# Decayed attention, a top-1 expert layer and a gated layer: three small edits that move work between VectorE, ScalarE and GpSimd

## The chip, the cores and the metric

The kernel runs on one core of a Trainium2 chip. The metric is device time of one execution in microseconds (us), as the median of three runs; lower is better. TensorE is called PE below, VectorE DVE, ScalarE ACT, GpSimd POOL and SyncE SP, as in the rows of the profile. PEld is the load of weights into TensorE, which runs beside its matmuls.

## The reference

Three layers follow one another. Sizes: B=4, H=8, S=576, D=64, so 2304 tokens of 512 numbers; 8 experts of width 1024; a gated layer of width 1536.

```python
def _attn_ref(q, k, v, f):
    scores = np.matmul(q, k.transpose(0, 1, 3, 2)) / np.sqrt(D)
    cum = np.cumsum(np.log(np.clip(f, 0.0001, 1.0)), axis=-1)
    scores = np.where(causal, -1000000000.0, scores + cum[:, :, :, None] - cum[:, :, None, :])
    return softmax(scores) @ v

def _moe_ref(x, modality_id, w_gate, modality_bias, w1, w2):
    logits = x @ w_gate + modality_bias[modality_id]
    e_idx = np.argmax(logits, axis=1)
    gate_w = softmax(logits)[np.arange(N), e_idx]
    for e in range(E):
        mask = e_idx == e
        out[mask] = gate_w[mask, None] * (np.maximum(x[mask] @ w1[e], 0.0) @ w2[e])

def _moe2_ref(x, w_gate, w_val, w_out):
    return (1.0 / (1.0 + np.exp(-(x @ w_gate))) * (x @ w_val)) @ w_out
```

## The kernel before

**Attention.** 32 heads are worked through one after the other, as 16 pairs. A head's step has scores on PE, a sum with the decay and a maximum on DVE (L249), exponentials on ACT (L257), transposes of the probabilities on PE (L268, L271), their high part on ACT (L278) and the low part on DVE (L279), the product with v (L336) and the sum over it that makes the rows of x and the logits (L367, L369, L550 on DVE, L551 on POOL). Matmuls work on a high and a low part of each number, so that each fp32 operand is split: a copy to the high part, then a subtraction for the low part. POOL builds the decay of the next head (`mask`, L183 and L187), and splits q, k and v of later heads (L147 to L167).

**Routing.** When the first half of the tokens has its logits (head 16 on), `early` picks two experts: `choose(0)` and `choose(1)` take the expert with most tokens, count at most 256 of them (`n`), and take them off the counts (`cnt`); `slots`, `ids` and `fetch` place these tokens and gather their rows. `finish` places all the others after the last head, with `place` called for all 18 token tiles (n == NTILE); `place` makes `hot`, a one-hot of the group, and `am`, `hot` times the tile's index and times the row's index, which a matmul with `bm` turns into lists of ids.

**Experts.** A unit is up to 256 tokens of one expert. Its weights come as 8 pieces of 128x1024, piece 2i from w1, piece 2i+1 from w2. `high` (L915 on POOL, L917 on ACT) and `low` (L923 on POOL or DVE) split a piece. Unit 0 uses buffers that attention leaves (`spare`): in rows of the trace eqd, ekd, esc, eph, epl are raw pieces or results of relu, and eq, ekh, ekl, edec are high and low parts. `pair` runs `up(f)` on PE (L989), `relu` (ACT L959 the high part, DVE L960 the low part) and, one step later, `down(f)` (L999). `up(f)` needs piece 2(f//2), `down(f)` piece 2(f//2)+1 and the result of relu f. In unit 0 the code splits pieces 0 to 3 in `begin` and pieces 4 to 7 in `step0`, and `POOL0` lists the pieces that POOL splits. Unit 1 follows with weights `ws`, split on ACT and DVE (wh, wl).

**What sets the order.** All of this up to unit 0 and `finish` is put in order by a scheduler when the program is built, from the order of the code and from its own estimates of when each operand is there; every engine then runs its list in order. From `rest` on the order is that of the code (`manual_schedule`).

Of the kernel before, what the change touches and what calls it, by code (L numbers as in the profile page):

```python
# [14 lines left out]
AF = mybir.ActivationFunctionType  # L15
ALU = mybir.AluOpType
# [4 lines left out]
P = 128  # L21
# [3 lines left out]
NTILE = NT // P  # L25
# [432 lines left out]
class Routing:  # L458
# [147 lines left out]
    def place(self, slot, add, g, ids):  # L606

        nc, V, tmp, n = self.nc, self.nc.vector, self.tmp, slot.shape[1]
        pi = tmp.tile([P, 3, n], I32, tag="pi", name="pi")
        dg = tmp.tile([P, 2, n], F32, tag="dg", name="dg")  # L610
        bm = tmp.tile([P, n, P], BF16, tag="bm" if n == NTILE else "xh0", name="bm")
        hot = tmp.tile([P, n, g], BF16, tag="hot", name="hot")
        am = tmp.tile([P, n, 2, g], BF16, tag="am", name="am")
        V.tensor_scalar(pi[:, 2], slot, add, None, ALU.add)
        V.tensor_scalar(pi[:, 0], pi[:, 2], 7, None, ALU.arith_shift_right)
        V.tensor_scalar(pi[:, 1], pi[:, 2], P - 1, None, ALU.bitwise_and)
        V.tensor_copy(dg, pi[:, 0:2])

        def onehot(o, digit, lanes):
            V.tensor_tensor(  # L620
                o, digit.unsqueeze(2).to_broadcast(o.shape), lanes.unsqueeze(1).to_broadcast(o.shape), ALU.is_equal
            )

        onehot(hot, dg[:, 0], self.grp[:, 0:g])
        nc.gpsimd.tensor_tensor(am[:, :, 0], hot, self.tix[:, 0:n].unsqueeze(2).to_broadcast([P, n, g]), ALU.mult)
        V.tensor_scalar(am[:, :, 1], hot, self.pix, None, ALU.mult)
        for i in range(0, n, 9):
            onehot(bm[:, i:i + 9], dg[:, 1, i:i + 9], self.lane)

        def collect(ps):  # L630
            for i in range(n):
                nc.tensor.matmul(ps, bm[:, i], am[:, i], start=(i == 0), stop=(i == n - 1))
            im = tmp.tile([P, 2, g], F32, tag="im", name="im")
            nc.scalar.activation(im, ps, AF.Copy)
            V.scalar_tensor_tensor(ids, im[:, 0], float(P), im[:, 1], ALU.mult, ALU.add)

        return collect

    def early(self):

        nc, V, wp = self.nc, self.nc.vector, self.wp
        t = lambda name, shape: wp.tile(shape, F32, tag=name, name=name)
        flat = lambda z: z.rearrange("p e o -> p (e o)")
        n0e, st = flat(self.n0e), {}

        def count():
            ps = self.ps_t.tile([P, 2, E, HT], F32, tag="t", name="t")
            st["rk"], st["cnt"] = self.ranks(ps, HT)

        def choose(i):  # L650

            cnt, mx, em, ne = flat(st["cnt"]), t("mx0", [P, 1]), t("em0", [P, 1]), t("ne0", [P, E])
            es, n = flat(self.es[i]), self.n0[:, i:i + 1]
            V.tensor_reduce(mx, cnt, AX.X, ALU.max)
            V.tensor_scalar(n, mx, 2.0 * P, None, ALU.min)
            V.tensor_scalar(es, cnt, n, None, ALU.is_ge)
            V.tensor_tensor(es, es, self.desc, ALU.mult)
            V.tensor_reduce(em, es, AX.X, ALU.max)
            V.tensor_scalar(es, self.desc, em, None, ALU.is_equal)
            V.tensor_scalar(self.te0[:, i:i + 1], em[0:1], -1.0, float(E), ALU.mult, ALU.add)  # L660
            ne = ne if i else n0e
            V.tensor_scalar(ne, es, n, None, ALU.mult)
            V.tensor_tensor(cnt, cnt, ne, ALU.subtract)
            if i:
                V.tensor_tensor(n0e, n0e, ne, ALU.add)

        def slots():

            rk, sel, off = st["rk"], t("sel", [P, E, HT]), t("off0", [P, E, 1])
            V.tensor_tensor(sel, rk, self.n0e.to_broadcast([P, E, HT]), ALU.is_lt)  # L670
            V.tensor_tensor(sel, sel, self.oh[:, :, 0:HT], ALU.mult)
            V.tensor_tensor(off, self.es[1], self.es[0], ALU.is_gt)
            V.tensor_scalar(off, off, 2.0 * P, -2.0 * P * NE, ALU.mult, ALU.add)
            V.tensor_tensor(rk, rk, off.to_broadcast([P, E, HT]), ALU.add)
            V.tensor_tensor(rk, rk, sel, ALU.mult)
            rr = t("rr", [P, HT])
            V.tensor_reduce(rr, rk.rearrange("p e t -> p t e"), AX.X, ALU.add)
            st["collect"] = self.place(rr, 2.0 * P * NE, 2 * NE, self.ids0)

        def ids():  # L680
            st["collect"](self.ps_t.tile([P, 2, 2 * NE], F32, tag="t", name="t"))
            pad, row = t("pad0", [P, 2]), t("row0", [P, 2])
            first, n = self.slot[:, 0:2], self.nt
            V.memset(n, 0.0)
            for i in range(NE):
                V.tensor_scalar(pad, first, self.n0[:, i:i + 1], None, ALU.is_ge)
                V.tensor_scalar(row, first, n, None, ALU.add)
                V.scalar_tensor_tensor(self.dst0[:, 2 * i:2 * i + 2], pad, float(2 * NT), row, ALU.mult, ALU.add)
                V.tensor_tensor(n, n, self.n0[:, i:i + 1], ALU.add)

        def fetch():
            for i, x in enumerate(self.xg):
                nc.gpsimd.indirect_dma_start(
                    out=x[:, :], out_offset=None, in_=self.xd[0:NT // 2],
                    in_offset=bass.IndirectOffsetOnAxis(ap=self.ids0[:, i:i + 1], axis=0),
                )

        return [count] + [lambda i=i: choose(i) for i in range(NE)] + [slots, lambda: None, ids, fetch] + self.then

    def finish(self, tmp, ps):  # L700
# [99 lines left out]
        V.tensor_tensor(row, self.slot, flat(of[:, 0]), ALU.add)  # L800
        V.scalar_tensor_tensor(self.dst, pad, float(2 * NT), row, ALU.mult, ALU.add)
        return lambda: place(ps.tile([P, 2, G], F32, tag="m", name="t", bufs=1))


class Experts:
# [2 lines left out]
    ORDER = [(0, 0), (1, 0), (0, 1), (1, 1), (0, 2), (1, 2), (0, 3), (1, 3)]  # L808


    POOL0 = 0, 1, 2, 4, 6
    SPARE = {"w": "kqkqcspr", "h": "2ldh2ldh", "l": "hd2lhd2l", "a": "kqkqkqkq"}

    def __init__(self, tc, ro, ps, xd, yd, w1, w2):
# [96 lines left out]
    def high(self, u, p):  # L911
        k = self.piece(u, p)
        hi = self.w[u, k] = self.part(u, p, "h")
        if u == 0 and p in self.POOL0:
            self.nc.gpsimd.tensor_scalar(hi, self.wraw(u, k), 1.0, 1.0, ALU.mult, ALU.mult)  # L915
# [3 lines left out]
    def low(self, u, p):  # L919
        k = self.piece(u, p)  # L920
        hi, lo = self.w[u, k], self.part(u, p, "l")
        eng = self.nc.gpsimd if u == 0 and p in self.POOL0 else self.nc.vector
        ins = eng.tensor_tensor(lo, self.wraw(u, k), hi.bitcast(F32), ALU.subtract)  # L923
# [471 lines left out]
```

## Time and profile before

| what | us |
|---|---|
| median of three runs | 998.96 (997.98 to 999.78) |
| the profiled execution | 1000.64 |
| its span, first to last instruction | 998.9 |
| PE busy in the span | 947.6 |
| DVE, ACT, POOL busy in the span | 576.1, 481.0, 298.3 |

The profiled execution is one run of the kernel, 1.74 us longer than its span and 1.68 us above the median. Times in rows count from the start of the span. Attention runs to about 267 us, unit 0 from there to 296, the other units to about 520, the gated layer to the end. PE has the most work; where it stops, the rows give in brackets how long it was idle and what ended that.

### The profile page before, as it was taken

What the parts mean: (1) busy time and instruction counts of PE and PEld (TensorE: products, weight loads), DVE (VectorE), ACT (ScalarE), POOL (GpSimd) and SP (SyncE); (2) the same over time, 40 slices, a digit from 0 to 9 for tenths busy, and PEclk for the clock granted to TensorE, in tenths of its full rate; (3) what the DMA queues carried; (4) which work ended last, traced back from release to release, by engine and by line L of the source; (5) the groups of instructions that cost most, each with busy time, mean ns of one, the idle gap of its engine ahead of it and who ended that gap; (6) DMA issues with size and microseconds to landing.
All of it is one profiled execution on the core that took longest, in us unless ns stands there. A gap on an engine that the chain in (4) does not pass through costs nothing. (4 is left out here: it accounts for less than half of the span.)

```text
span 998.9 us, 16941 instructions
## 1 busy us (share of the span) xinstructions
PE 947.6 (95%) x5871; PEld 878.9 (88%) x5871; DVE 576.1 (58%) x1494; ACT 481.0 (48%) x1058; POOL 298.3 (30%) x563
## 2 busy tenths in 40 slices
PE   4999999889979999999989998999999999999996
PEld 4899998789868999999879887999999999999995
DVE  7988889888796889898766682122122122122111
ACT  5889888678436666666664442122122122112111
POOL 6999998879422222211000001001001001001001
PEclk8999999999999999999999998999999999999998
DMA  6545547344354394345732220001001001000000
GB/s 141 136 124 132 130 111 135 87 104 157 103 178 128 108 304 137 112 134 176 243 132 75 84 95 32 1 1 64 1 1 64 1 1 64 1 1 32 1 1 32
DMA packets 95486, 88.98 MB, mean 89 GB/s; under 512 B 47456, under 2 KB 78688, under 8 KB 95392
## 3 DMA queue, kind: packets, MB, share of 16 engines
q1 hardware_dynamic: 90752, 73.12, 26.2%
q0 software_dynamic: 4640, 14.70, 4.2%
q8 instruction: 48, 0.79, 0.3%
q14 instruction: 46, 0.38, 0.1%
HBM read 98.72 MB, written 14.77 MB: 114 GB/s over the span
## 5 line engine op out<-in xcount | busy, mean ns | idle before, releaser
L1226 PE MATMUL g<-xh,gh 128*128 128x384 f32 x576 | 195.5, 339 | 3.3 <-PEq L1354 3.1
L1226 PE MATMUL g<-xl,gh 128*128 128x384 f32 x576 | 193.8, 336 | 0.0
L1233 DVE TENSOR_TENSOR s<-s,g 128x384 f32<-128x384 f32 x72 | 39.8, 553 | 257.5 <-PE g L1226 257.5
L1226 PE MATMUL g<-xh,bits 128*128 128x384 f32 x528 | 177.6, 336 | 1.7 <-DVE bits L1175 1.6
L1259 POOL DMA_INDIRECT out_dram<-os,tok x18 | 17.5, 973 | 458.1 <-ACT os L1258 456.3
L1226 PEld LDWEIGHTS g<-xh,gh 128*128 128x128 f32 x576 | 108.6, 189 | 5.9 <-ACTq L1354 3.5
L1234 ACT ACTIVATE ah<-s 128x384 fp32r<-128x384 f32 x72 | 37.8, 525 | 157.5 <-DVE s L1233 157.5
L1226 PEld LDWEIGHTS g<-xl,gh 128*128 128x128 f32 x576 | 108.7, 189 | 1.8
L1232 ACT ACTIVATE s<-g 128x384 f32<-128x384 f32 x72 | 35.3, 490 | 140.2 <-PE g L1226 137.2
L1226 PEld LDWEIGHTS g<-xh,bits 128*128 128x128 f32 x528 | 99.1, 188 | 2.9 <-DVE bits L1175 2.9
L923 DVE TENSOR_TENSOR wl<-ws,wh 128x1024 fp32r<-128x1024 f32 x80 | 97.2, 1216 | 3.3 <-ACT hr L1032 2.3
L257 ACT ACTIVATE sc<-sc,mn 128x576 f32<-128x576 f32 (+4 forms) x160 | 89.3, 562 | 14.0 <-DVE mn L249 13.2
L917 ACT ACTIVATE wh<-ws 128x1024 fp32r<-128x1024 f32 x80 | 84.4, 1056 | 18.7 <-PE y L999 17.2
L1244 PE MATMUL o<-gh,ah 128*128 128x512 f32 x216 | 85.9, 398 | 3.6 <-ACT gh L1174 3.6
L183 POOL TENSOR_SCALAR dec<-cum 128x576 f32<-128x576 f32 (+4 forms) x160 | 84.5, 540 | 4.2 <-DMA cum<-drow 4.0
L1244 PE MATMUL o<-gh,al 128*128 128x512 f32 x216 | 84.7, 392 | 0.0
L969 POOL DMA_INDIRECT rows_by_expert<-ys,dst x20 | 23.8, 1188 | 180.3 <-ACT ys L968 94.4
L989 PE MATMUL h<-xh,wh 128*128 128x256 f32 x256 | 73.9, 289 | 0.0
L1244 PE MATMUL o<-gl,ah 128*128 128x512 f32 x180 | 71.3, 396 | 2.0 <-DVE gl L1175 2.0
L989 PE MATMUL h<-xl,wh 128*128 128x256 f32 x256 | 72.5, 283 | 0.4 <-DVE xl L944 0.4
L989 PE MATMUL h<-xh,wl 128*128 128x256 f32 x256 | 72.6, 284 | 0.0
L279 DVE TENSOR_TENSOR pl<-t,ph 128x512 fp32r<-128x512 f32 x96 | 65.0, 679 | 11.5 <-ACT ph L278 10.7
(301 smaller groups left out, 2364.7 us busy)
## 6 DMA issues: line engine op xcount, KB each, us to landing
ws<-in_moe_w_dram SPq DMA_DIRECT2D x80, 512.0 KB
cum<-drow SPq DMA_DIRECT2D x32, 288.0 KB
raw<-in_moe_w_gate_dram SPq DMA_DIRECT2D x12, 512.0 KB
raw<-in_moe_w_val_dram SPq DMA_DIRECT2D x12, 512.0 KB
raw<-in_moe_w_out_dram SPq DMA_DIRECT2D x12, 512.0 KB
y<-rows_by_expert SPq DMA_DIRECT2D x18, 256.5 KB
qr<-in_q_dram SPq DMA_DIRECT2D x32, 128.0 KB
kd<-in_k_dram SPq DMA_DIRECT2D x32, 128.0 KB
```

The lines of the kernel that those rows point to most:

```text
L183: nc.gpsimd.tensor_scalar(t[0:m, DO[b]:DO[b] + W[b]], c[0:m, 0:W[b]], -1.0, c[0:m, R0[b]:R0[b] + 1], ALU.mult, ALU.add)
L257: nc.scalar.activation(so, so, AF.Exp, bias=mn[0:m, b:b + 1], scale=-1.0, accum_out=sm[0:m, c:c + 1])
L279: nc.vector.tensor_tensor(pl[0:m, o:o + w], t, ph[0:m, o:o + w].bitcast(F32), ALU.subtract)
L917: self.nc.scalar.activation(hi, self.wraw(u, k), AF.Copy)
L923: ins = eng.tensor_tensor(lo, self.wraw(u, k), hi.bitcast(F32), ALU.subtract)
L969: nc.gpsimd.indirect_dma_start(out=self.put[g], out_offset=bass.IndirectOffsetOnAxis(ap=dst[:, j:j + 1], axis=0), in_=ys[:, :], in_offset= ...
L989: nc.tensor.matmul(t, a[:, c, cs], b[:, c, :], start=(n == 0), stop=(n == 3 * KD - 1))
L1226: nc.tensor.matmul(t, p[:, c, :], q[:, c, :], start=(n == 0), stop=(n == 3 * KD - 1))
L1232: nc.scalar.activation(s, ps[0], AF.Sigmoid)
L1233: nc.vector.tensor_tensor(s, s, ps[1], ALU.mult)
L1234: nc.scalar.activation(hi, s, AF.Copy)
L1244: nc.tensor.matmul(o[j], p[:, cs], q, start=(f == 0 and n == 0), stop=(f == self.NF - 1 and n == 2))
```

## The change

Three edits. In `choose`, the row `ne = es * n` (one number per expert, 128x8) is made by ACT in place of DVE, in both calls. In `place`, the product that makes the first half of `am` is made by DVE in place of POOL when it is called for all 18 tiles; the early call with 9 tiles stays on POOL. And POOL splits pieces 0, 1, 2, 3 of unit 0 where it split 0, 1, 2, 4, 6: piece 3 goes from ACT and DVE to POOL, pieces 4 and 6 from POOL to ACT and DVE.

```diff
         onehot(hot, dg[:, 0], self.grp[:, 0:g])
-        nc.gpsimd.tensor_tensor(am[:, :, 0], hot, self.tix[:, 0:n].unsqueeze(2).to_broadcast([P, n, g]), ALU.mult)
+        (V if n == NTILE else nc.gpsimd).tensor_tensor(am[:, :, 0], hot, self.tix[:, 0:n].unsqueeze(2).to_broadcast([P, n, g]), ALU.mult)
...
             ne = ne if i else n0e
-            V.tensor_scalar(ne, es, n, None, ALU.mult)
+            nc.scalar.activation(ne, es, AF.Copy, scale=n)
             V.tensor_tensor(cnt, cnt, ne, ALU.subtract)
...
-    POOL0 = 0, 1, 2, 4, 6
+    POOL0 = 0, 1, 2, 3
```

The scheduler then orders the lists anew. On DVE in `choose(1)` (rk_3211 is `cnt`; L249 is attention's sum and maximum, L279 the low part of probabilities):

```order
 L660 TENSOR_SCALAR te_77<-em_3499 1x1
 L279 TENSOR_TENSOR pl_142<-t,ph_141 128x512
-L662 TENSOR_SCALAR ne_3500<-es_89,n_90 128x8
-L249 ISA sc_137,mn<-s,dec 64x64
-L249 ISA mn 64x1
 L663 TENSOR_TENSOR rk_3211<-rk_3211,ne_3500 128x8
 L665 TENSOR_TENSOR n0e<-n0e,ne_3500 128x8
+L249 ISA sc_137,mn<-s,dec 64x64
+L249 ISA mn 64x1
 L279 TENSOR_TENSOR pl_142<-t,ph_141 128x512
 L249 ISA sc_137,mn<-s,dec 128x448
```

L662 is gone from the list, and the two subtractions that need its result stand ahead of attention's L249, not behind it.

On POOL at the end of attention (eqd, ekd here are raw pieces 1 and 3, 0 and 2; esc is piece 4, eph piece 6):

```order
 L923 TENSOR_TENSOR edec<-eqd,ekl 128x1024
 L551 TENSOR_TENSOR lg<-lt,lg 128x24
+L915 TENSOR_SCALAR ekh<-eqd 128x1024
+L923 TENSOR_TENSOR ekl<-eqd,ekh 128x1024
 L915 TENSOR_SCALAR edec<-ekd 128x1024
 L923 TENSOR_TENSOR eq_4734<-ekd,edec 128x1024
 L551 TENSOR_TENSOR lg<-lt,lg 128x24 x6
-L915 TENSOR_SCALAR eq_4780<-esc_4703 128x1024
-L923 TENSOR_TENSOR ekh_4782<-esc_4703,eq_4780 128x1024
-L915 TENSOR_SCALAR edec<-eph_4705 128x1024
-L923 TENSOR_TENSOR eq_4834<-eph_4705,edec 128x1024
-L625 TENSOR_TENSOR am<-hot,tix 128x18x27
```

Piece 3 is split between pieces 1 and 2, and after the last L551 POOL has no compute left in unit 0.

On DVE in the middle of unit 0, around relu of f=3 (L960), before:

```order
L766 SCALAR_TENSOR_TENSOR pl_4990<-gs,n0e 128x8
L742 TENSOR_REDUCE tef<-past 1x27
L768 SCALAR_TENSOR_TENSOR pl_4992<-c,gs 128x8
L772 TENSOR_TENSOR rk_4942<-rk_4942,pl_4990 128x144
L746 COPY own<-tef 1x7
L747 COPY own<-tef 1x9
L769 TENSOR_TENSOR pl_4992<-pl_4992,gs 128x8
L923 TENSOR_TENSOR edec<-esc_4704,ekl 128x1024
L960 SCALAR_TENSOR_TENSOR eqd<-h,eqd 128x256
```

and there in the changed kernel:

```order
L766 SCALAR_TENSOR_TENSOR pl_4990<-gs,n0e 128x8
L742 TENSOR_REDUCE tef<-past 1x27
L923 TENSOR_TENSOR edec<-esc_4704,ekl 128x1024
L960 SCALAR_TENSOR_TENSOR eqd<-h,eqd 128x256
L923 TENSOR_TENSOR eq_4834<-eph_4705,edec 128x1024
L746 COPY own<-tef 1x7
L747 COPY own<-tef 1x9
```

The low part of relu f=3 stands five rows of `finish` earlier, and the low part of piece 6 follows it. In the same way relu f=7 now stands ahead of the last rows of `finish` (L793 to L801, the list `dst`), where it stood behind them.

## Rows read from the trace of the kernel before

**Rows 1.** The page's first line, the span.
```profile
span 998.9 us, 16941 instructions
```

**Rows 2.** PE timeline: start us, us, instruction, [idle before <-releaser].
```profile
195.14 1.56 PE L367 MATMUL t<-iw,ot 128*128 128x72 f32 x6 [2.90 <-DVE pl L279]
...
258.84 0.67 PE L367 MATMUL t<-iw,ot 128*128 128x72 f32 x4 [1.51 <-DVE ot L354]
...
281.94 0.73 PE L999 MATMUL y<-ekh,eqd 128*128 128x512 f32 x2 [2.81 <-DVE eqd L960]
...
289.73 0.73 PE L999 MATMUL y<-ekl,eqd 128*128 128x512 f32 x2 [1.90 <-DVE eqd L960]
...
298.64 0.38 PE L989 MATMUL h<-xl,wh 128*128 128x256 f32 x1 [0.41 <-DVE xl L944]
```

**Rows 3.** Stretches: us, busy by engine (count), PEclk granted, DMA share, GB/s.
```profile
192.24:195.14 2.90, 0.01 (x1) 0.00 (x0) 2.90 (x7) 1.45 (x5) 2.14 (x5) 1.00 0.50 129
195.14:202.08 6.94, 6.94 (x34) 6.72 (x34) 4.11 (x23) 3.14 (x9) 4.33 (x12) 0.51 0.21 50
260.05:263.31 3.26, 3.26 (x15) 3.07 (x15) 1.64 (x7) 1.09 (x3) 0.23 (x1) 0.50 0.66 220
290.78:294.18 3.40, 3.40 (x16) 3.22 (x14) 2.65 (x9) 0.60 (x2) 0.00 (x0) 0.51 0.56 199
```

**Rows 4.** A stretch later on, columns as in Rows 3 (PE, PEld, DVE, ACT, POOL).
```profile
320.00:340.00 20.00, 20.00 (x131) 18.11 (x130) 16.08 (x28) 13.28 (x21) 5.39 (x4) 1.00 0.33 106
```

**Rows 5.** DVE timeline around choose(1) and the routing rows after it.
```profile
190.53 3.01 DVE L662 TENSOR_SCALAR ne<-es,n 128x8 f32<-128x8 f32 x1
...
201.37 0.21 DVE L320 RECIPROCAL r<-r 128x9 f32<-128x9 f32 x1 [2.81 <-ACT r L319]
...
217.72 0.89 DVE L686 TENSOR_SCALAR pad<-slot,n 128x2 f32<-128x2 f32 x1
```

**Rows 6.** POOL timeline over the time of L662, and its wait after 200.
```profile
190.69 0.72 POOL L187 TENSOR_SCALAR_AFFINE_SELECT dec<-dec 128x128 f32<-128x128 f32 x3
191.39 0.86 POOL L167 TENSOR_TENSOR vv<-vr,vv 128x320 fp32r<-128x320 f32 x1
...
193.05 0.45 POOL L166 TENSOR_SCALAR vv<-vr 128x320 fp32r<-128x320 f32 x1
...
204.53 0.49 POOL L166 TENSOR_SCALAR vv<-vr 128x320 fp32r<-128x320 f32 x1 [3.94 <-PE m L336]
```

**Rows 7.** ACT timeline: a small row, and the high part of piece 3.
```profile
201.14 0.20 ACT L319 ACTIVATE r<-sm 128x9 f32<-128x9 f32 x1
...
251.60 1.06 ACT L917 ACTIVATE ekh<-eqd 128x1024 fp32r<-128x1024 f32 x1
```

**Rows 8.** DVE timeline: the low part of piece 3, then unit 0.
```profile
255.12 3.40 DVE L923 TENSOR_TENSOR ekl<-eqd,ekh 128x1024 fp32r<-128x1024 f32 x1
...
271.26 2.50 DVE L716 TENSOR_TENSOR cmp<-rk,thr 128x144 f32<-128x144 f32 x1
...
274.69 0.28 DVE L770 TENSOR_TENSOR half<-rk,pl 128x144 f32<-128x144 f32 x1
...
277.11 2.29 DVE L766 SCALAR_TENSOR_TENSOR pl<-gs,n0e 128x8 f32<-128x8 f32 x1
...
280.35 1.21 DVE L923 TENSOR_TENSOR edec<-esc,ekl 128x1024 fp32r<-128x1024 f32 x1
...
285.47 0.66 DVE L620 TENSOR_TENSOR hot<-dg,grp 128x486 bf16<-128x486 f32 x1
...
287.32 2.02 DVE L923 TENSOR_TENSOR ekl<-epl,ekh 128x1024 fp32r<-128x1024 f32 x1
```

**Rows 9.** POOL timeline: the low part of piece 6.
```profile
276.75 2.62 POOL L923 TENSOR_TENSOR eq<-eph,edec 128x1024 fp32r<-128x1024 f32 x1
```

**Rows 10.** Unit 0 from relu f=0 to f=7, columns as in Rows 3.
```profile
268.88:294.42 25.54, 20.83 (x122) 17.94 (x121) 24.49 (x72) 5.54 (x11) 9.19 (x5) 0.93 0.50 140
```

**Rows 11.** The rows for dst, columns as in Rows 3.
```profile
291.46:293.40 1.94, 1.94 (x11) 1.94 (x11) 1.79 (x7) 0.00 (x0) 0.00 (x0) 0.50 0.56 195
```

## The prediction

> **What bounds the kernel now.** I began with the stretches. From 320 us on PE is busy for 20.00 of 20 us at full granted clock [rows 4], and its later waits are between engines that follow PE, so whatever is won before 300 us should reach the end as it is. The loss that this change can touch lies ahead of that, in three places, each found by PE's own idle rows and then by the engine that they name.
>
> Place A, `choose(1)`. PE waits 2.90 us for a low part L279 on DVE [rows 2], and DVE is then in L662, 3.01 us for eight numbers per partition [rows 5]. POOL runs one instruction after the other through that time, from L187 at 190.69 to L166, which ends at 193.50 [rows 6], and L662 ends at 193.54. So DVE stood behind POOL's whole train. After it PE's granted clock is 0.51, near its lower level of 1.2 GHz, for 6.94 us [rows 3]; work at half pace loses half of that, 3.4 us. Place A costs 2.9 + 3.4 = 6.3 us.
>
> Place B, the end of attention. PE waits 1.51 us for L354 on DVE [rows 2], which stands behind the low part of piece 3: 3.40 us [rows 8], where the same operation and shape takes 1.21 at 280.35 [rows 8]. Then 3.26 us at granted clock 0.50 [rows 3] lose 1.6. Place B costs 3.1.
>
> Place C, unit 0. PE waits 2.81 and 1.90 us for low parts L960 on DVE [rows 2], and 3.40 us at 0.51 [rows 3] lose 1.7: together 6.4. DVE is the bound here: from relu f=0 to relu f=7 it is busy for 24.49 of 25.54 us [rows 10]. Part of this is again POOL: L716 takes 2.50 where L770, of the same 144 columns and also with two inputs in SBUF, takes 0.28; L766 takes 2.29 for 8 columns [rows 8] and ends at 279.40, as POOL's low part of piece 6 ends at 279.37 [rows 9]; the low part of piece 7 takes 2.02 against 1.21 [rows 8].
>
> **The change part by part.** *ne on ACT.* It removes L662 from DVE. On ACT it is one small row; the nearest, 128x9, takes 0.20 [rows 7], and ACT has no work while DVE stands. L663 now waits for it, and behind L663 in DVE's list are L665 and attention's L249. Both subtractions read two SBUF inputs, so they can stand behind POOL too. At best each waits for nothing, at worst for the 3 us that L662 waited. I take one POOL row each, by the longest of the train, 0.86 [rows 6], less what is idle between: about 1 us for both, so that PE's wait shrinks from 2.9 to under 1. What follows limits the gain. DVE was idle for 2.81 us at 201 [rows 5] because PE was slow, and POOL for 3.94 us up to 204.53 [rows 6], so the small routing rows of `slots` ran free of it. If all moves up, those rows meet a busy POOL, as L686 does, with 0.89 us for two columns [rows 5]. Bounds for A: nothing (the wait passes to L663) and 6.3. I take 2.6, which is 6.3 less about 1 for the subtractions and less some four such meetings of 0.7 us.
>
> The Trainium skill, page "SBUF — State Buffer", section "Who interferes with whom", says that VectorE contends with GpSimd for one pair of ports when it runs in a 2-port mode or reads two SBUF inputs, and that whoever starts first keeps it for its whole instruction. The lengthened rows of place C agree with that; L662 does not, since it stood behind five and more GpSimd instructions and not one. By the page a wait is worth at most one GpSimd row, so A would come to some 0.8 us and the sum below to 7.8; by the row it is 3.01 us.
>
> *Piece 3 to POOL.* DVE loses 3.40 us and ACT 1.06 [rows 7, 8], at a place where both stand before PE's last head. POOL gets the two instructions ahead of piece 2, a copy and a subtraction, the longer no more than the 2.62 of piece 6 [rows 9]. Pieces 2 and 3 are first read in up(2) and down(2), behind up(0), up(1) and down(0), and these hide it; without that cover up(2) would wait for up to twice 2.62. The bounds for B are nothing (the last head's chain of exponentials, copies and products is as long as the wait that goes) and 3.1 plus the 1 us by which ACT is earlier. I take 3.0.
>
> *Pieces 4 and 6 to ACT and DVE, am to DVE.* ACT gets 2 x 1.06 us, and it is busy for 5.54 of 25.54 there [rows 10]: no cost, unless its waits for a buffer hold the relu behind them. DVE gets 2 x 1.21 for the low parts, and am, for which `hot` with the same 486 elements and two inputs is the nearest row, 0.66 [rows 8]: 3.1 us. POOL has then no compute left, so L716 loses 2.2, L766 at least 2.0 (to L770's 0.28) and the low part of piece 7 0.8: 5.0 us off. By the new order the rows for dst, 1.8 us [rows 11], move behind relu f=7. DVE thus needs 24.5 - 5.0 + 3.1 - 1.8 = 20.8 us where it took 25.5, and relu f=7 comes 4.7 us earlier, with PE's stops, now within that, gone or short. PE alone could win 6.4. But the 1.8 us come back ahead of unit 1's weight splits and of the low part of x that PE awaited at 298.64 [rows 2]: by that 4.7 - 1.8 = 2.9 is left, and by PE's stops alone 6.4 - 1.8 = 4.6. I take 4.0, nearer to the second, since PE's stops end with a stretch at half clock that goes with them. Below both lies nothing, if DVE's rows do not shrink. The weights `ws` of unit 1 are loaded once piece 5 is split and once down(5) is done; both come earlier by the order shown, so SP's queue is no new wait.
>
> **Sum.** 2.6 + 3.0 + 4.0 = 9.6 us. Against the profiled execution's own 1000.64 us (span 998.9 [rows 1] and 1.74 around it) that is 991.0; the profile lies 1.68 above the median of 998.96, and against the median it is 989.4. I say **989.5**.
>
> **The rivals.** *The wait is only handed on.* L663 or a routing row behind it runs into POOL's train as L662 did, and A brings nothing. For it speaks that POOL is busy in the same way around it [rows 6]; against it, that nothing else in the shown rows waits for more than one or two instructions of POOL. The Trainium skill's page, named above, speaks against it as well, with one instruction as the longest wait. The time would be 998.96 - 7.0 = 992.0. Chance 0.17.
>
> *Unit 0 is bound by DVE's own list.* Its rows shrink less, or the rows for dst and two weight splits ahead of unit 1 make PE wait as long as before, with a new stretch at half clock. Then C brings nothing or 1, and A and B stay: 998.96 - 5.6 = 993.4, or up to 992.4. For it speaks that DVE keeps 20.8 us of work there; against it the 5.0 us measured behind POOL. Chance 0.12.
>
> *Little moves.* A and C bring nothing and the last head's chain takes B: 998 to 1000. It needs all three, chance 0.06.
>
> *New trains (slower).* The routing rows after `choose(1)`, which ran while POOL was idle for 3.94 us [rows 6], now stand in a full POOL stream. Each that meets a train as long as L662's costs PE 2.9 us idle and 3.4 at half clock, 6.3. One such meeting is A's gain undone; two cost 12.6 against at most 6.3 + 3.0 + 4.0 = 13.3, no change; from three on, 18.9, the kernel is slower by 5.6: 1004.6. Only one row of the trace is that long at such a place, L662, and L686 with 0.89 is the usual kind. Chance 0.04.
>
> **How the numbers follow.** The forecast has what is left, 0.61, and its own range is 985 to 991.5. The predicted time is its likeliest value. A measurement of this kernel tells about 0.2%, 2 us. Faster by more than that hold the forecast, the first rival and the second: 0.90; same is "little moves": 0.06; slower 0.04. The range reaches down to all that the three places cost, 6.3 + 3.1 + 6.4 = 15.8, with the 1 us more in B and less the 1.8 us that come back, 15.0, so 984.0, and up to the second rival with part of its C lost again, 996; beyond lie the last two rivals, with 0.10, and some 0.08 below or between.
>
> **What the changed profile would show.** For A: L662 on ACT at about 0.2 us, L663 and L665 under 1 us each on DVE, and no idle row of PE over 1 us near 192, nor a stretch at 0.5 behind it. For B: no L923 on DVE before unit 0, L354 behind L279 at once, and PE at full clock up to unit 0. For C: L716 and L766 at 0.3 us or less, low parts of pieces 4 to 7 at 1.21 each on DVE, PE without idle rows over 0.5 us between up(0) and down(7), then a wait of 2 to 3 us for unit 1's xl. That xl matmul, at 298.64 before, should stand at about 289. The prediction is wrong if L716 or L766 are as long with POOL idle, if L663 takes L662's 3 us, or if relu's low parts still hold PE.

## The result, and the profile after

The changed kernel takes **989.18 us** (median of four, 987.4 to 990.08) against 999.37 for the kernel before beside it; ratio 0.9896 (0.9869 to 0.9923). The forecast was 989.5. Run again beside other kernels it took 989.87 of 999.01, ratio 0.9909 (0.9882 to 0.9936). The profiled execution took 987.4 us:

```profile
span 985.7 us, 16946 instructions
```

That is 13.2 us under the span of [rows 1], more than the medians' 10.2: one execution of each kernel is compared here, and both kernels spread by several us. PE's timeline of the changed kernel, which answers to [rows 2]:

```profile
183.75 0.33 PE L271 MATMUL t<-swp,sc 128*128 128x128 f32 x1 [1.37 <-DVE pl L279]
193.73 0.33 PE L271 MATMUL t<-swp,sc 128*128 128x128 f32 x1 [0.94 <-DVE pl L279]
...
201.57 0.28 PE L198 MATMUL t<-idr,qd 128*128 128x128 f32 x1 [0.47 <-DVE kl L204]
206.44 0.89 PE L367 MATMUL t<-iw,ot 128*128 128x72 f32 x6 [0.49 <-DVE kl L204]
...
285.88 0.39 PE L989 MATMUL h<-xl,wh 128*128 128x256 f32 x1 [2.37 <-DVE xl L944]
```

Places B and C are clean: no row of PE waits between 221 and 283 us, where it waited for 1.51, 2.81 and 1.90 us, and the matmul for xl stands at 285.88, where it stood at 298.64. The 2.37 us in front of it are the wait forecast there. Unit 0 on DVE, as in [rows 8]:

```profile
263.19 0.30 DVE L716 TENSOR_TENSOR cmp<-rk,thr 128x144 f32<-128x144 f32 x1
...
267.52 0.14 DVE L766 SCALAR_TENSOR_TENSOR pl<-gs,n0e 128x8 f32<-128x8 f32 x1
...
273.37 1.20 DVE L923 TENSOR_TENSOR ekl<-epl,ekh 128x1024 fp32r<-128x1024 f32 x1
...
278.47 0.66 DVE L625 TENSOR_TENSOR am<-hot,tix 128x486 bf16<-128x486 bf16 x1
```

L716 fell from 2.50 to 0.30, L766 from 2.29 to 0.14, piece 7 from 2.02 to 1.20, and `am` takes the 0.66 that `hot` took. One row more got shorter, L737, which I had not counted; before, on DVE's timeline,

```profile
275.94 1.19 DVE L737 TENSOR_TENSOR past<-grp,gs 128x432 f32<-128x432 f32 x1
```

and in the changed kernel:

```profile
266.94 0.59 DVE L737 TENSOR_TENSOR past<-grp,gs 128x432 f32<-128x432 f32 x1
```

Place A is another matter. `choose(1)` on DVE and POOL of the changed kernel:

```profile
190.24 2.79 DVE L659 TENSOR_SCALAR es<-desc,em 128x8 f32<-128x8 f32 x1
...
193.60 0.14 DVE L663 TENSOR_TENSOR rk<-rk,ne 128x8 f32<-128x8 f32 x1
193.68 0.15 DVE L665 TENSOR_TENSOR n0e<-n0e,ne 128x8 f32<-128x8 f32 x1
```

```profile
190.62 0.72 POOL L187 TENSOR_SCALAR_AFFINE_SELECT dec<-dec 128x128 f32<-128x128 f32 x3
191.31 0.85 POOL L167 TENSOR_TENSOR vv<-vr,vv 128x320 fp32r<-128x320 f32 x1
192.13 0.23 POOL L551 TENSOR_TENSOR lg<-lt,lg 128x24 f32<-128x24 f32 x1
192.34 0.67 POOL L152 TENSOR_SCALAR kd<-kd 128x576 f32<-128x576 f32 x1
```

L663 and L665 (both called subtractions above; L665 is an addition) are free, but L659, three rows ahead of L663, now stands behind the same train of POOL, its rows one right after the other, for 2.79 us. PE's wait is 0.94 us all the same, and no half clock follows it. A stretch at half clock came earlier instead, behind the 1.37 us at 183.75 (stretches, columns as in Rows 3):

```profile
184.00:190.00 6.00, 6.00 (x40) 5.74 (x39) 5.08 (x21) 4.06 (x14) 4.88 (x9) 0.72 0.33 75
193.00:203.00 10.00, 8.78 (x67) 7.92 (x68) 9.40 (x43) 8.02 (x25) 6.18 (x17) 1.00 0.21 56
```

So the total fits and two of its three terms stand; whether the third does, one profile can't say.

### The profile page after: what moved, and what is told of

Same layout as the page of the kernel before. It is cut to its first block, busy times and chain, and to the rows that moved or that the text cites. A ratio compares the mean times of both kernels' runs of the same rounds, so it can differ in the third digit from the quotient of the medians.

```text
span 985.7 us, 16946 instructions
## 1 busy us (share of the span) xinstructions
PE 940.9 (95%) x5871; PEld 872.7 (89%) x5871; DVE 567.4 (58%) x1494; ACT 482.1 (49%) x1061; POOL 291.4 (30%) x560
## 5 line engine op out<-in xcount | busy, mean ns | idle before, releaser
L989 PE MATMUL h<-xl,wh 128*128 128x256 f32 x256 | 72.4, 283 | 2.4 <-DVE xl L944 2.4
L989 PE MATMUL h<-xh,wh 128*128 128x256 f32 x256 | 73.7, 288 | 0.0
L989 PE MATMUL h<-xh,wl 128*128 128x256 f32 x256 | 72.6, 284 | 0.0
L279 DVE TENSOR_TENSOR pl<-t,ph 128x512 fp32r<-128x512 f32 x96 | 65.0, 679 | 11.6 <-ACT ph L278 10.7
```

The costliest lines, as they stand in the source:

```text
L279: nc.vector.tensor_tensor(pl[0:m, o:o + w], t, ph[0:m, o:o + w].bitcast(F32), ALU.subtract)
L989: nc.tensor.matmul(t, a[:, c, cs], b[:, c, :], start=(n == 0), stop=(n == 3 * KD - 1))
```

## Experiments

The theory to be tested was that of the prediction, with A in doubt: three places add up, A by `ne`, B by piece 3, C by pieces 4 and 6. The rival was its first rival, that A's wait is only handed on. All times below are medians beside the kernel before on the same chip; 0.001 of the ratio is 1 us. The ratio, with its 95% interval, is not the quotient of the two medians and can differ from it by up to 1.7 us (piece 6 on POOL). Every edit lets the scheduler order the lists anew, so each run shows its edit together with the new order. For each profile I also took three lengths from the timelines. **S0** runs from ACT's copy of a finished head (L349, at 183.77 in the kernel before) to that at 231.20, five heads on, around `choose(1)`. **S1** runs on from there to the first matmul of unit 0 (L989), and **S2** from that to the first xl of unit 1 on DVE (L944). In the kernel before:

```profile
231.20 0.60 ACT L349 ACTIVATE ot<-o 128x512 f32<-128x512 f32 x1 [0.30 <-PE o L336]
...
266.67 0.36 PE L989 MATMUL h<-xh,eq 128*128 128x256 f32 x1
...
297.89 0.69 DVE L944 TENSOR_TENSOR xl<-x,xh 128x512 fp32r<-128x512 f32 x1 [0.27 <-ACT im L634]
```

and in the changed kernel:

```profile
227.33 0.60 ACT L349 ACTIVATE ot<-o 128x512 f32<-128x512 f32 x1 [0.29 <-PE o L336]
...
258.89 0.37 PE L989 MATMUL h<-xh,eq 128*128 128x256 f32 x1
...
285.14 0.68 DVE L944 TENSOR_TENSOR xl<-x,xh 128x512 fp32r<-128x512 f32 x1
```

| kernel | S0 | S1 | S2 | ratio to before |
|---|---|---|---|---|
| before | 47.43 | 35.47 | 31.22 | 1 |
| `ne` alone | 42.90 | 37.03 | 29.66 | 0.9997 (0.9978 to 1.0015) |
| `am` alone | 45.07 | 37.05 | 28.85 | 0.9973 (0.9951 to 0.9994) |
| piece 3 to POOL alone | 45.13 | 31.54 | 31.25 | 0.9951 (0.9935 to 0.9967) |
| piece 4 off POOL alone | 47.74 | 33.89 | 27.64 | 0.9962 (0.9945 to 0.9980) |
| new list alone | 47.31 | 31.57 | 26.24 | 0.9891 (0.9861 to 0.9921) |
| the same again | 45.13 | 31.56 | 26.24 | 0.9903 (0.9884 to 0.9923) |
| list and `am` | 45.15 | 31.55 | 26.40 | 0.9896 (0.9866 to 0.9927) |
| list and `ne` | 44.29 | 31.54 | 26.09 | 0.9882 (0.9854 to 0.9910) |
| the same again | 45.50 | 31.57 | 26.06 | 0.9892 (0.9873 to 0.9911) |
| changed kernel | 43.54 | 31.56 | 26.25 | 0.9896 (0.9869 to 0.9923) |
| the same again | 44.27 | 31.56 | 26.24 | 0.9909 (0.9882 to 0.9936) |
| changed, piece 6 on POOL | 43.34 | 31.54 | 27.68 | 0.9914 (0.9890 to 0.9939) |
| changed, rows for dst later | 46.66 | 31.53 | 24.14 | 0.9941 (0.9921 to 0.9960) |

A length is read from one execution. S0 of the kernel before and of the changed kernel, columns as in Rows 3 (PE's idle time is the length less PE's busy time):

```profile
183.77:231.20 47.43, 41.88 (x302) 39.34 (x303) 41.88 (x151) 33.17 (x95) 37.52 (x78) 0.89 0.47 111
```

```profile
183.79:227.33 43.54, 39.80 (x302) 36.47 (x303) 40.53 (x150) 32.91 (x96) 36.63 (x75) 0.96 0.50 114
```

 What is left of the span behind S2 is 698.8 to 704.0 us in all rows but the last, with or without the gains ahead of it: so these reach the end, but within a spread of 5 us.

**`ne` alone.**

```diff
-            V.tensor_scalar(ne, es, n, None, ALU.mult)
+            nc.scalar.activation(ne, es, AF.Copy, scale=n)
```

> The kernel before with one edit of the change alone: the chosen row's `ne` on ScalarE. Nothing is left out. My theory: in the kernel before, choose(1) holds up the heads behind it through its DVE row L662 (3.01 us) and the half clock that follows PE's 2.90 us wait; with `ne` on ACT the row takes 0.3 us and PE's wait near 193 falls under 1.5 us without a half clock behind it, so 2.6 to 4 us are gained: about 996 us, ratio 0.996 to 0.998. The rival (the wait is only handed on to the next row that DVE writes while POOL's train runs, and PE waits as long as before): L659 or L663 near 190 to 194 takes the 3 us instead, PE's row at 195 stays at 2.5 us or more, and the ratio is within 0.002 of 1.

It took 999.96 us against 999.85: nothing, as the rival says, though the interval leaves room for 2.2 us. The DVE timeline shows the wait handed on, to L663 here, and PE's timeline what it costs:

```profile
191.94 2.56 DVE L663 TENSOR_TENSOR rk<-rk,ne 128x8 f32<-128x8 f32 x1
```

```profile
195.37 0.89 PE L367 MATMUL t<-iw,ot 128*128 128x72 f32 x6 [1.97 <-DVE pl L279]
202.29 0.28 PE L198 MATMUL t<-idr,qd 128*128 128x128 f32 x1 [0.47 <-DVE kl L204]
207.18 0.89 PE L367 MATMUL t<-iw,ot 128*128 128x72 f32 x6 [0.51 <-DVE kl L204]
```

The wait fell from 2.90 to 1.97, and two new ones of 0.47 and 0.51, behind L204 on DVE, take the place of smaller ones: those of PE's idle times that the view shows, from here to the head at 228, add up to 4.85 us, and from the same place in the kernel before to 5.55. So the idle time won is 0.7 us. In this execution no half clock followed, and S0 is 4.53 us shorter; but the stretch from 250 to 260 was granted 0.80, S1 is 1.56 longer, and the time is no better.

**The new list alone, and the change without `ne`.**

```diff
-    POOL0 = 0, 1, 2, 4, 6
+    POOL0 = 0, 1, 2, 3
```

> The kernel before with the list of p pieces for POOL set to 0, 1, 2, 3 alone; `ne` and `am` stay where they were. Nothing is left out. My theory: this is where most of the gain comes from, the end of attention and unit 0: 6.5 to 8 us, about 992 us, ratio 0.992 to 0.9935, with L716 and L766 in unit 0 at 0.1 to 0.3 us instead of 2.3 to 2.5, the row for L662 at 3 us and PE's half clock behind 195 us as before. The rival (unit 0 is bound by DVE's own list, which p6's and p7's splits make longer): only the attention part is gained, 3 to 4 us, ratio 0.996, and DVE's last split ends as late after f0 as in the kernel before.

> The changed kernel without one edit: `ne` stays on DVE. Nothing is left out. My theory: choose(1) costs what it did before (L662 3 us, PE's wait near 195 us at 2.5 us or more and a half clock behind it), and the rest of the gain stays: 6 to 8 us, about 992.5 us, ratio 0.992 to 0.994. The rival (the wait near choose(1) is handed on anyway): no difference from the changed kernel, ratio 0.9895.

The list alone took 989.91 us and with `am` 989.09: the whole gain, by the ratios 10.9 and 10.4 us and so more than the theories' 6 to 8 (the intervals reach down to 7.9 and 7.3). That leaves no room for the rival of the first, and is what the rival of the second says. In both, L662 stood for 3 us and PE for 2.90 us in `choose(1)` as before.

**`am` alone.**

```diff
-        nc.gpsimd.tensor_tensor(am[:, :, 0], hot, self.tix[:, 0:n].unsqueeze(2).to_broadcast([P, n, g]), ALU.mult)
+        (V if n == NTILE else nc.gpsimd).tensor_tensor(am[:, :, 0], hot, self.tix[:, 0:n].unsqueeze(2).to_broadcast([P, n, g]), ALU.mult)
```

> The kernel before with `am` (the routing product of the last units) on DVE alone. Nothing is left out. My theory: this row, 0.6 to 0.9 us on either engine, decides nothing by itself: ratio within 0.001 of 1. The rival: POOL's `am` is one of the rows behind which DVE's rows of unit 0 wait, and without it up to 1 us is gained, ratio 0.999.

997.23 us, 2.7 less by the ratio (0.6 to 4.9): more than the theory allows, though the interval reaches down to it, and the rival has the mechanism; its 1 us lies in the interval. In the kernel before, POOL's `am` took 2.06 us from 286.21, not the 0.6 to 0.9 that I had put, and DVE's low part of piece 7 beside it 2.02 [rows 8]. Without it, on DVE's timeline:

```profile
289.00 1.22 DVE L923 TENSOR_TENSOR ekl<-epl,ekh 128x1024 fp32r<-128x1024 f32 x1
```

PE's wait of 1.90 us behind it is gone and S2 is 2.37 shorter. But not all of that is the work of `am`. In `ne` alone, where unit 0 has the same list for POOL and the same rows as in the kernel before, S2 is 1.56 shorter too, and that wait is 0.61 on PE's timeline:

```profile
288.24 0.73 PE L999 MATMUL y<-ekl,eqd 128*128 128x512 f32 x2 [0.61 <-DVE eqd L960]
```

There the half clock follows the first of unit 0's two waits (granted 0.60 from 280.47 to 284.00), in the kernel before the second. In `am` alone it follows the first as well (0.59 from 283.64 to 287.20), so the S2 to compare with is that of `ne` alone, and it is 0.81 shorter.

**Pieces 3 and 4, one at a time.**

```diff
-    POOL0 = 0, 1, 2, 4, 6
+    POOL0 = 0, 1, 2, 3, 4, 6
```

> The kernel before with p3 alone moved to POOL: POOL splits p0, p1, p2, p3, p4, p6. Nothing is left out. It is to measure the end of attention by itself. Theory: DVE's 3.40 us for p3's low at 255.12 goes, PE's wait of 1.51 us at 258.84 and the half clock behind it go with it, and unit 0 starts 3 to 4 us earlier; unit 0 itself keeps its waits (L716, L766, PE's 2.81 us): 995.5 to 997 us, ratio 0.996 to 0.997. Rival (the two parts are one wait: unit 0 starts earlier, but its end hangs on DVE and POOL as before, so that PE only waits longer for eqd): under 1 us, ratio 0.999 or more.

```diff
-    POOL0 = 0, 1, 2, 4, 6
+    POOL0 = 0, 1, 2, 6
```

> The kernel before with p4 alone moved to DVE: POOL splits p0, p1, p2, p6. Nothing is left out. It is to measure unit 0 by itself. Theory: L716 comes down from 2.5 to 0.3 us, since POOL's split of p4 no longer runs beside it, DVE's 1.2 us for p4 are less than that, and PE's two waits in unit 0 shrink from 4.7 us to under 2.5 us; the end of attention stays as it was: 994.5 to 996.5 us, ratio 0.995 to 0.997. Rival (only p6's place counts, or DVE's list is the bound): ratio 0.999 or more.

Piece 3 alone took 993.95 us: 4.9 off by the ratio (3.3 to 6.5), more than expected. S1 fell by 3.93 and S2 stayed to 0.03, so B is a place of its own; the waits of unit 0 are all there in PE's timeline:

```profile
275.26 0.73 PE L999 MATMUL y<-ekh,eqd 128*128 128x512 f32 x2 [2.82 <-DVE eqd L960]
```

Piece 4 alone took 996.02 us, 3.8 off (2.0 to 5.5), as expected, and S2 fell by 3.58 (2.02 against `ne` alone). Piece 6, still on POOL, now holds a third row, L748, as the POOL and the DVE timeline show:

```profile
277.09 2.55 POOL L923 TENSOR_TENSOR eq<-eph,edec 128x1024 fp32r<-128x1024 f32 x1
```

```profile
277.31 2.36 DVE L748 TENSOR_SCALAR rev<-own 1x18 f32<-1x18 f32 x1
```

The two together are 8.7 us by the ratios, the list 9.7 to 10.9.

**Piece 6 back on POOL.**

```diff
-    POOL0 = 0, 1, 2, 3
+    POOL0 = 0, 1, 2, 3, 6
```

> The changed kernel with one more piece for POOL: p6 back on it, so that DVE splits p4, p5, p7 and POOL p0, p1, p2, p3, p6. Nothing is left out. Theory: what the new list gives in unit 0 comes from DVE's rows no longer standing behind POOL's split of p6: L766 is 2.2 to 2.4 us long again beside that split, but DVE has 1.2 us less of its own, so the first row of unit 1 for PE comes 0 to 2 us later: 989 to 991 us. Rival (unit 0 is bound by the sum of DVE's rows, and the row that waits costs nothing): it is faster than the changed kernel by 1.2 us, 988 us.

988.75 us, no difference from the changed kernel's 989.87 that could be told, so neither side is decided by the time. S2 is 1.43 longer, by the same 2.4 us in L748 less the 1.2 us that DVE no longer has; L766 was free, against what I expected. The wait fell to the row that DVE came to when POOL's long row had begun: L766 in the kernel before, L748 in these two.

**`ne` within the new list.**

```diff
-        (V if n == NTILE else nc.gpsimd).tensor_tensor(am[:, :, 0], hot, self.tix[:, 0:n].unsqueeze(2).to_broadcast([P, n, g]), ALU.mult)
+        nc.gpsimd.tensor_tensor(am[:, :, 0], hot, self.tix[:, 0:n].unsqueeze(2).to_broadcast([P, n, g]), ALU.mult)
```

This is the changed kernel with `am` back on POOL; the list alone differs from it in `ne` only.

> The changed kernel itself, once more, beside the runs that follow. Nothing is left out. The four runs so far put `ne` alone at no difference and the new list for POOL alone at 0.989, about the whole gain. Theory now: `ne` brings forward the heads behind choose(1) by 3 us or more, but the new list alone has most of the gain, so the changed kernel comes within 1.5 us of the kernel without `ne`: 988 to 990.5 us, ratio 0.989 to 0.991. Rival (the three edits add up, and 3.9 us of choose(1) show in the time): 985 to 986.5 us, ratio 0.986.

> The changed kernel with `am` back on POOL. Nothing is left out. Theory: 0.7 us of POOL's time at 278 us in front of DVE's last rows of unit 0, which PE's wait for unit 1 hangs on; 0 to 1 us over the changed kernel, about 989.8 us. Rival (what `am` alone gave on the kernel before, 2.6 us, is its own worth in either kernel): 991.5 us or more.

> The changed kernel with `am` back on POOL once more, beside the same kernel without `ne` on ACT (the next run): the pair differs in `ne` alone. Nothing is left out. Theory: `ne` is worth about 1 us here, less than the 2 us by which profiles with it come through choose(1) earlier on average: 986.5 to 989 us. It is also the fastest median so far (987.3 us); the rival is that this was the spread of five runs, and that it comes out at 989 to 990 us as the changed kernel does.

> The kernel before with POOL's list set to 0, 1, 2, 3 alone once more, the other half of the pair. Nothing is left out. Theory: 1 us behind the run before it, 988 to 990 us, ratio 0.989 to 0.991. Rival 1 (`ne` is worth nothing in the time): within 0.5 us of it. Rival 2 (`ne` is worth what the profiles show, 3 us): 990.5 us or more.

The first time list and `ne` took 987.32 us, the fastest median of all; beside the list alone it took 989.54, and that 988.62. So it is no better version, as the rival had it, and the 1 us that I expected of `ne` did not show: none of these kernels with the new list can be told from another by its time. All 18 executions with the list and without `ne` have a median of 989.4 us, the 21 with both 989.2; resampled, the difference lies between -2.5 and +0.8 (they come from several chips). `am`, with which the kernel before was 2.7 us faster, shows no gain here: piece 7's low part is over before POOL begins with it.

**The rows for dst later.** In the changed kernel the last 2 us of DVE rows for dst stand ahead of the splits of unit 1 and of xl; the earlier ones stand within unit 0. All of them, 4.8 us in 17 rows, are put into a function `rows`, which is called ahead of unit 0's last step (the rest of the edit is cut here):

```diff
         self.high(1, 3)
+        rows()
         for _ in self.run0:
```

> The changed kernel with the rows that work out `dst` (2.3 us of DVE between 280.9 and 282.9 us and behind) written behind the last splits of unit 0 and ahead of its last step, so that xl of unit 1 and the wl pieces come ahead of them. Nothing is left out. Theory: in the changed kernel PE's longest wait left is the 2.37 us for xl at 285.88 us, behind the rows for dst and two wl of 2.36 us; with the rows later it falls by about 2 us, 987 us, ratio 0.9875. Rival: xl stays behind the two wl, or the rows only come back ahead of the next thing PE needs, and nothing changes: 989 us.

992.41 us, 2.5 slower than the changed kernel beside it, each of its eight executions (from 991.18) above each of the other's six (to 990.9). PE's timeline has both halves of the answer:

```profile
286.17 0.39 PE L992 MATMUL h<-xl,wh 128*128 128x256 f32 x1 [0.34 <-DVE xl L947]
...
293.85 0.80 PE L1002 MATMUL y<-wh,hl 128*128 128x512 f32 x1 [3.86 <-DVE hl L963]
```

The wait for xl fell by the 2 us of the theory, from 2.37 to 0.34, and a new one of 3.86 stands 8 us on, for the low part of unit 1's relu, which stands behind the rows for dst on DVE, with one small cast between (first row, last row, relu):

```profile
288.34 0.16 DVE L782 SCALAR_TENSOR_TENSOR q<-c,rk 128x8 f32<-128x8 f32 x1
...
293.15 0.19 DVE L802 SCALAR_TENSOR_TENSOR dst<-pad,row 128x27 int32<-128x27 f32 x1
...
293.38 0.41 DVE L963 SCALAR_TENSOR_TENSOR hl<-h,hh 128x256 fp32r<-128x256 f32 x1
```

That is the rival's second half, and it costs more than it gave.

## Why the prediction was right, point by point

**The total.** 989.5 against 989.18. It holds because A was too large, and B and probably C too small. That the errors cancel to 0.3 us is luck; that the gain lies at B and C is not.

**A, 2.6 us: failed.** The step that fell is "I take one POOL row each", for L663 and L665. A row that comes next stands behind the train and not behind one row of it: L663 for 2.54 to 2.56 us in five profiles with `ne` on ACT, L659 for 2.79 in the changed kernel (in its second profile the two share it, 1.31 and 1.00, and PE's wait is 0.38). Not every run of POOL's rows holds one so long: L659 took 0.52 at 189.44 in the kernel before, where POOL was as busy. What makes the difference is not shown. That L663 takes L662's time was one of the prediction's own signs of being wrong, and in those five profiles it took 2.5 us of them. Against the first rival I had said that no other row waits so long; it was right about the mechanism, and wrong in its 992.0 only since B and C are larger.

What A brings in the time is -0.1 us alone (2.2 at most) and 0.2 within the list (2.5 at most). In the profiles S0 is shorter by 1.8 us with `ne`: 44.4 on average of seven profiles, the one with dst later among them (46.66), against 46.1 of seven without. The spread on both sides is 2.7 to 3.8. Part of it is the half clock, which comes in some executions and not in others: the granted clock of S0 is 0.89 to 0.96 without `ne` and 0.89 to 1.00 with it. PE's idle time in S0 tells the two sides apart: 5.54 to 5.87 us in the seven without `ne`, 3.14 to 5.07 in the seven with it, 1.4 less on average. So some of the wait does go; whether that 1.4 us reaches the time, the runs do not settle. The second part of A that failed is its 3.4 us of half clock, taken as if it came each time.

**B, 3.0: right in mechanism, undersized.** S1 is 31.53 to 31.57 us in each of ten profiles with piece 3 on POOL, and 33.89 to 37.05, on average 35.9, in the four without, the shortest of them without a half clock behind PE's wait: 4.3 us, and 4.9 in the time. I had the extra 1 us by which ACT is earlier as a bound and left it out of the value. The copies of heads L349 were 6.97 us apart in the kernel before where ACT had piece 3's copy between them (246.34 to 253.31), and 6.03 in the changed one.

**C, 4.0: right in mechanism, probably undersized.** S2 fell by 4.97 us (by 3.41 against `ne` alone, by 5.00 against piece 3 alone): 4.71 of PE's two waits and 1.7 of the half clock, less 1.96 by which the wait for xl grew (2.37 against 0.41), are 4.5 of it. In the time, the list less piece 3 alone is 4.8 to 6.0. The 1.8 us for dst that I took as coming back did so, by PE's wait almost to the number. By DVE's list the sizes were otherwise: from relu f=0 to the end of relu f=7 it took 25.54 us before and 19.86 after, 5.7 less where I had 4.7, and L737 with its 0.6 is part of what I had missed; from there to xl it took 3.47 and 4.17, 0.7 more where I had 1.8, since DVE's waits for ACT on that way (0.52, 0.23 and 0.27) went. That the weight lay with POOL's rows and not with DVE's list is shown by piece 4 alone, which puts 1.2 us on DVE's list and shortens S2 by 3.58 (2.02 against `ne` alone), and by `am` alone, which puts 0.66 on it and shortens S2 by 0.81 against `ne` alone.

**The second rival** (unit 0 bound by DVE's own list) falls with these two. "New trains" did not come: the routing rows after `choose(1)` gave PE two waits of half a us.

**The Trainium skill's page "SBUF — State Buffer"**, section "Who interferes with whom", has the first comer keep the port for its whole instruction. In unit 0 the rows agree: L748 ends with POOL's one row, after 2.36 us. In `choose(1)` L662, L663 and L659 each outlast a train of several POOL rows, and there the measurement decides. That a wait is one row at most was my reading of the rule; the section does not say what a row waits for when several rows of the other engine follow one another. My estimate of 0.8 us by it was nearer to what A brought in the time than my 2.6, but not for its reason, the wait being no shorter than the train.

## What to carry to other kernels

A row that waits for another engine's train can be only the next in line. Before costing its removal at the whole wait, look at what stands next in the same list while the train still runs; here, taking rows off POOL (pieces 4 and 6) removed the waits of unit 0, and moving the row that waited (`ne`) handed most of its wait on. And where an engine is full up to a deadline, putting its rows off can move the stall to the next deadline: PE's stall was 2.37 us with the rows for dst where they were, and 0.34 and 3.86 with them later.

## What I had not expected of the hardware

A stretch at half clock need not follow the same wait each time. The kernel with list and `ne` was profiled twice, with PE waits of 1.98 and 1.97 us at 193, and its stretch behind them was granted 0.83 and 0.66. First one, then the other:

```profile
193.00:203.00 10.00, 9.30 (x57) 8.39 (x58) 8.20 (x36) 7.20 (x23) 5.90 (x15) 0.83 0.20 54
```

```profile
193.00:203.00 10.00, 9.37 (x50) 9.10 (x50) 7.13 (x29) 6.28 (x17) 5.43 (x14) 0.66 0.21 56
```

Over one set of 23 executions of the kernel before, times ran from 994.8 us at a mean granted clock of 0.989 to 1005.7 at 0.977. The wait in `choose(1)` itself repeats to a few hundredths of a us in each kernel profiled there with the same row held (2.86 to 2.90 in seven profiles without `ne`, 1.96 to 1.99 in five with it), but not in the changed kernel (0.94 and 0.38). So here a stall could be costed by its idle time, and the half clock behind it only as something that comes in part of the executions. My 3.4 us for it in place A was one such draw.

The sharing goes both ways: POOL's copy of piece 6 (L915) took 1.05 us in the kernel before, and 2.49 us in the one with piece 4 off POOL, where DVE's low part of piece 5 ran beside it.
